# Attention on one Trainium2 core: the value products of a round in two PSUM banks instead of one, the first scores over all eight

## The chip, the cores and the metric

The kernel runs on one core of a Trainium2 chip. Its engines work side by side, each through its own list of instructions in order: TensorE (PE: matrix products and transposes, into PSUM), VectorE (DVE), ScalarE (ACT), GpSimd (POOL), and SyncE (SP), which here only issues DMAs. PSUM has eight banks of 2 KB in each of 128 partitions; the kernel names them h0 to h3 and y0 to y3. The metric is the device time of one execution in microseconds (us). The kernel before takes 863.77 us (median of three runs, 863.53 to 864.34).

## The reference

What is computed is an attention with a causal window of 128 positions, followed by two feed-forward layers:

```
scores = q k^T / 8 - slope_h * |i - j|   for 0 <= i - j < 128, else -1e9   (4 batches, 8 heads, 576 positions, 64 wide)
attn   = softmax(scores); x = attn v            -> x: 2304 tokens x 512
x      = (x w_in) * cos(x w_in) w_out           (512 -> 2048 -> 512)
out    = gate(x w_in') w_out'                   (the same sizes, a piecewise square)
```

All of it is in fp32. The change touches only how the attention is laid out in PSUM and in what order its steps are issued.

## The kernel before

**Pairs and rounds.** The 2304 tokens are 18 blocks of 128. A *pair* is two neighbouring blocks (j = 0, 1) with two heads (h = 0, 1); there are 36 pairs, and two of them (k = 0, 1) make a *round*: 18 rounds, r = 0 to 17. For a pair the kernel does the following.

1. `score`: four matmuls, q of block j against the 256 (at a sequence's start 128) keys before it. The scores of one head lie in one bank, those of block 0 in its columns 0 to 255, those of block 1 behind them. Then for each j and h a DVE operation (L493) adds the distance table, takes the row's extreme and writes the scores to SBUF (a tile `sc`), and ACT takes the exponential in place (L498).
2. `normal`: a sum gets 1e-9 added (L506), DVE takes the reciprocal (L507), and POOL multiplies the scores by it (L517), one instruction for each block.
3. `turn_round`: PE transposes each block's `sc` (L534) into a bank, and DVE or ACT copies that to SBUF (L541, a tile `pt`; of three copies two on DVE).
4. `output`: PE multiplies `pt` by v (L559). The result is x. For the first 768 tokens (pairs 0 to 11, so rounds 0 to 5) it stays in SBUF as a rounded high part (ACT, L577) and the remainder (DVE, `sub_lo` at L296), the second from the first; for later tokens one engine copies it (L587) and SP stores it.

**Order on PE.** It is the order of the program: in turn r come the scores of round r (banks y0 to y3), the products with v of round r-2 (both pairs in bank h3, pair 1 behind pair 0), and the transposes of round r-1 (h0, h1 for pair 0; h2, h3 for pair 1). Turn r is the stretch from one round's scores to the next round's. The scores of round 0 alone lie in h0 to h3.

**Order on the other engines.** A planner (`Plan.order`, with a cost and a latency for each operation in `COST`) runs the whole program through a model and fixes the order in which DVE, ACT, POOL and SP get their instructions. Operations depend on each other by resources: a bank, a buffer, and before the change also the two column ranges of a bank as resources of their own (`p["part"]`, `parts`). Semaphores are set by the layer below, by tiles of PSUM.

**After the attention** the feed-forward layers begin with `mm_a` (L754) into h0, h1 and h3, their activations (L763 to L778) and `mm_b` (L793); the last two products with v and the last transposes lie between these. From there on the kernel is a long row of 128x128x384 matmuls (L870, L942, L1031), with weights decoded on ACT and DVE, stored and loaded again (`wq`).

Of the kernel before, what the change touches and what calls it, by code (L numbers as in the profile page):

```python
# [9 lines left out]
F32 = mybir.dt.float32  # L10
# [247 lines left out]
def attention_moe_moe_kernel(  # L258
# [40 lines left out]
    def big(tag, bufs, name, dtype=F32R, shape=(128, 2, 512)):  # L299
        return two.tile(list(shape), dtype, tag=tag, name=nm(name), bufs=bufs)  # L300
# [129 lines left out]
    def attention(plan, bank, x_res, sin_ready, stat, dist_held):  # L430
# [3 lines left out]
        for name in ("straddle", "after"):  # L434
            for i in range(2):
# [17 lines left out]
        def stats(p, a, b):  # L453
            return stat.t.rearrange("p k n -> p (k n)")[:, 12 * p["n"] + a:12 * p["n"] + b]

        def used(o):
            if o not in stat.users:
                stat.users.append(o)
            return o
# [4 lines left out]
            p[name] = b = Buf("B", lambda: big("B", 14, name, F32, (128, 2 * HT)))  # L464
            op("S", name, lambda: SP.dma_start(b.t[:, 0:c.stop - c.start], qkv[p["b0"] // 2, p["hp"], :, c]), writes=[b], gate=gate)

        def score(p, j, tags, first):
            w = p["w"][j]
            kc = 256 + (j + 2) * 128 - w
            if j == 0:  # L470
                p["bank"] = [Cell(), Cell()]
                p["part"] = [[Res(), Res()] for _ in range(2)]
            cells, b = p["bank"], p["qk"]

            def go():
                for h in range(2):
                    if j == 0:
                        cells[h].t = ps.tile([128, 512], F32, tag=tags[h], name=nm("pa"))
                for h in range(2):
                    r = slice(64 * h, 64 * h + 64)  # L480
                    PE.matmul(cells[h].t[:, 256 * j:256 * j + w], lhsT=b.t[r, j * 128:j * 128 + 128],  # L481
                              rhs=b.t[r, kc:kc + w], start=True, stop=True)

            o = op("PE", "s+" if first else "s", go, reads=[b],
                   writes=[*p["part"][j], *([bank[t] for t in tags] if j == 0 else [])])
            sc = Buf("s", lambda: small("sc", shape=(128, 2, 256)))
            p["sc", j] = sc, [Half(sc), Half(sc)]
            for h in range(2):
                part = lambda: cells[h].t[:, 256 * j:256 * j + w]
                area = lambda h=h: cells[h].t[:, 256 * j:256 * j + w]  # L490
                res = p["part"][j][h]
                c = 2 * j + h
                o = op("D", f"max{w}", lambda a=area, h=h, c=c: DVE.tensor_tensor_reduce(  # L493
                    out=sc.t[:, h, 0:w], in0=a(), in1=dist8[p["kind"][j], 2 * p["hp"] + h][:, 256 - w:256], scale=-0.125,
                    scalar=3.0e38, op0=ALU.add, op1=ALU.min, accum_out=stats(p, c, c + 1)),
                    reads=[res, bank[tags[h]], *far.get((p["kind"][j], p["hp"] // 2), ())], writes=[p["sc", j][1][h]])
                maxes.append(used(o))
                exps.append(used(op("A", f"exp{w}", lambda h=h, c=c: ACT.activation(  # L498
                    sc.t[:, h, 0:w], sc.t[:, h, 0:w], AF.Exp, bias=stats(p, c, c + 1), scale=-1.0,
                    accum_out=stats(p, 4 + c, 5 + c)), writes=[p["sc", j][1][h]])))  # L500

        def normal(p, near):
            g = exps[-4:]
# [20 lines left out]
        def turn_round(p, j, tag, first, e=None):  # L524
            nb, n = p["w"][j] // 128, 2 * p["w"][j]
            sc, hs = p["sc", j]
            cell = Cell()

            def go():
                cell.t = ps.tile([128, 512], F32, tag=tag, name=nm("pa"))  # L530
                for h in range(2):
                    for i in range(nb):
                        c = (h * nb + i) * 128
                        PE.transpose(cell.t[:, c:c + 128], sc.t[:, h, i * 128:i * 128 + 128], ident)  # L534

# [5 lines left out]
            op(e, f"pt{n}", lambda: f(b.t[:, 0:n], cell.t[:, 0:n]), reads=[bank[tag]], writes=[b])  # L541

        moved = [0]

        def output(ps_, tag, e=None):
            cell, parts = Cell(), [Res(), Res()]
            for k, p in enumerate(ps_):

                def go(k=k, p=p):
                    if k == 0:  # L550
                        cell.t = ps.tile([128, 512], F32, tag=tag, name=nm("pa"))
                    for j in range(2):
                        nb = p["w"][j] // 128
                        for i in range(nb):
                            for h in range(2):
                                vc = (j + 2 - nb + i) * 128 + 64 * h
                                c = (h * nb + i) * 128
                                o = 256 * k + 128 * j
                                PE.matmul(cell.t[64 * h:64 * h + 64, o:o + 128],  # L559
                                          lhsT=p["v"].t[:, vc:vc + 64], rhs=p["pt", j].t[:, c:c + 128],  # L560
                                          start=(i == 0), stop=(i == nb - 1))

                op("PE", "v" if k else "v+", go, reads=[p["v"], p["pt", 0], p["pt", 1]],
                   writes=[parts[k], *([] if k else [bank[tag]])])
            for k, p in enumerate(ps_):
                src = lambda k=k: cell.t[:, 256 * k:256 * k + 256]
                t0, hp = p["b0"] * 128, p["hp"]
                if t0 < CH:
                    i = int(t0 >= FIRST[1][0])
                    c = t0 - FIRST[i][0]  # L570
                    hi, lo = Res(), Res()
                    x_res[i, hp] += [hi, lo]

                    def high(i=i, hp=hp, c=c, src=src):
                        if (i, hp) not in x0:
                            new_x0(i, hp)
                        ACT.copy(x0[i, hp][0][:, c:c + 256], src())  # L577

                    op("A", "x256", high, reads=[parts[k], bank[tag]], writes=[hi])
                    op("D", "x256", lambda i=i, hp=hp, c=c, src=src: sub_lo(  # L580
                        DVE, x0[i, hp][1][:, c:c + 256], src(), x0[i, hp][0][:, c:c + 256]),
                        reads=[parts[k], bank[tag], hi], writes=[lo])
# [4 lines left out]
                op(f, "x256", lambda x=x, f=f, src=src: (ACT.copy if f == "A" else DVE.tensor_copy)(x.t, src()),  # L587
                   reads=[parts[k], bank[tag]], writes=[x])
# [701 lines left out]
```

## Time and profile before

| what | value |
|---|---|
| median of three runs | 863.77 us (863.53 to 864.34) |
| the profiled execution | 864.19 us, span 862.1 us |
| PE / DVE / ACT / POOL busy over the span | 98% / 83% / 75% / 10% |
| attention, from round 0's scores to those of round 17 | 4.03 to 102.76 us |

The profile is of one execution. The span is what the profiler recorded, 2.1 us less than that execution's time. PE is busy for nearly all of the span; what is left to gain on waits is the rest, and where PE waits can be read from the idle time ahead of an instruction and what released it.

### The profile page before, as it was taken

What the parts mean: (1) busy time and instruction counts of PE and PEld (TensorE: products, weight loads), DVE (VectorE), ACT (ScalarE), POOL (GpSimd) and SP (SyncE); (2) the same over time, 40 slices, a digit from 0 to 9 for tenths busy, and PEclk for the clock granted to TensorE, in tenths of its full rate; (3) what the DMA queues carried; (4) which work ended last, traced back from release to release, by engine and by line L of the source; (5) the groups of instructions that cost most, each with busy time, mean ns of one, the idle gap of its engine ahead of it and who ended that gap; (6) DMA issues with size and microseconds to landing.
All of it is one profiled execution on the core that took longest, in us unless ns stands there. A gap on an engine that the chain in (4) does not pass through costs nothing.

```text
span 862.1 us, 16046 instructions
## 1 busy us (share of the span) xinstructions
PE 846.5 (98%) x5376; PEld 812.0 (94%) x5376; DVE 717.6 (83%) x1657; ACT 644.1 (75%) x1430; POOL 83.0 (10%) x118
## 2 busy tenths in 40 slices
PE   6999999999999999999999999999999999999998
PEld 5778878888889999999999999999999999999998
DVE  6889899899878998989888977877779999488954
ACT  6899878999857787677777767775488866488652
POOL 4877730000000000000000000000000000000000
PEclk9999999999999999999999999999999999999999
DMA  8678646785789998679889599999499898887861
GB/s 322 190 230 280 192 160 230 247 281 192 264 300 360 354 385 308 241 275 356 275 307 345 188 335 339 382 373 328 135 310 337 316 357 294 296 283 268 314 211 56
DMA packets 107730, 241.71 MB, mean 280 GB/s; under 512 B 10368, under 2 KB 57472, under 8 KB 107648
## 3 DMA queue, kind: packets, MB, share of 16 engines
q1 hardware_dynamic: 107648, 240.69, 79.7%
q8 instruction: 43, 0.70, 0.3%
q14 instruction: 39, 0.32, 0.1%
HBM read 174.59 MB, written 63.96 MB: 277 GB/s over the span
## 4 chain that ended last, share of the span: by engine, by line
PE 93%; DVE 3%; ACT 2%; POOL 1%; issue 1%; DMA 0%; POOLq 0%; ACTq 0%; DVEq 0%
PE h L870 34%; PE y L942 23%; PE y L1031 13%; PE y L793 8%; PE h L754 7%; PE pa L481 3%; PE pa L559 2%; PE pa L534 2%; DVE sc L493 1%; ACT sc L498 1%; POOL sc L517 1%; DVE pt L541 0%; DMA qk<-in_qkv 0%; ACT x L577 0%; DVE x L296 0%
## 5 line engine op out<-in xcount | busy, mean ns | idle before, releaser
L870 PE MATMUL h<-b,wq 128*128 128x384 f32 x1680 | 302.0, 334 | 0.6 <-ACT c L878 0.6
L870 PEld LDWEIGHTS h<-b,wq 128*128 128x128 f32 x1680 | 292.0, 188 | 1.0 <-ACT c L878 0.9
L942 PE MATMUL y<-gh,wo 128*128 128x384 f32 x768 | 203.4, 334 | 0.0
L942 PEld LDWEIGHTS y<-gh,wo 128*128 128x128 f32 x768 | 139.5, 188 | 0.0
L942 PE MATMUL y<-gl,wo 128*128 128x384 f32 x384 | 128.3, 334 | 0.0
L1031 PE MATMUL y<-gs,wq 128*128 128x384 f32 x672 | 118.1, 334 | 0.0
L1031 PEld LDWEIGHTS y<-gs,wq 128*128 128x128 f32 x672 | 116.6, 188 | 0.0
L883 DVE TENSOR_TENSOR c<-h,c 128x384 f32<-128x384 f32 x136 | 75.0, 555 | 39.6 <-ACT c L878 24.7
L878 ACT COPY c<-h 128x384 f32<-128x384 f32 x120 | 57.3, 478 | 51.2 <-PE h L870 49.9
L498 ACT ACTIVATE sc<-sc,up 128x256 f32<-128x256 f32 (+1 forms) x144 | 70.1, 488 | 13.9 <-DVE up L493 12.5
L1059 ACT CAST gs<-g 128x384 fp32r<-128x384 f32 x96 | 49.3, 513 | 33.9 <-PE y L1031 31.7
L517 POOL TENSOR_TENSOR sc<-sc,up 128x512 f32<-128x512 f32 (+1 forms) x71 | 70.8, 1019 | 26.1 <-DVE up L507 21.2
L754 PE MATMUL h<-x,wi 128*128 128x512 f32 (+1 forms) x384 | 72.2, 338 | 0.1
L942 PEld LDWEIGHTS y<-gl,wo 128*128 128x128 f32 x384 | 72.1, 188 | 0.0
L754 PEld LDWEIGHTS h<-x,wi 128*128 128x128 f32 x384 | 60.0, 190 | 8.3 <-ACT x L587 0.3
L296 DVE TENSOR_TENSOR gs<-g,gs 128x384 fp32r<-128x384 f32 x96 | 53.4, 557 | 16.6 <-ACT gs L1059 16.3
L493 DVE CUSTOM_DVE_ANT_0 sc<-pa,dist 128x256 f32<-128x256 f32 (+1 forms) x144 | 50.5, 402 | 8.1 <-PE pa L481 8.0
L903 ACT ACTIVATE t<-t,values 128x384 f32<-128x384 f32 x64 | 39.3, 615 | 11.5 <-DVE t L900 10.5
L296 DVE TENSOR_TENSOR so<-up,so 128x512 fp32r<-128x512 f32 x64 | 41.7, 655 | 3.7 <-ACT so L334 3.6
L534 PE MATMUL pa<-ident,sc 128*128 128x128 f32 x272 | 36.8, 281 | 6.8 <-POOL sc L517 2.8
L667 ACT ACTIVATE wst<-wst 128x512 int32<-128x512 uint16 x64 | 42.7, 670 | 0.0
L675 DVE TENSOR_SCALAR wst<-wst 128x512 uint16<-128x512 uint16 x55 | 42.3, 773 | 0.5
(96 smaller groups left out, 1345.1 us busy)
## 6 DMA issues: line engine op xcount, KB each, us to landing
wq<-fd SPq DMA_DIRECT2D x120, 512.0 KB, 5.8
wst<-in_w SPq DMA_DIRECT2D x64, 512.0 KB, 4.9
wq<-foM SPq DMA_DIRECT2D x56, 512.0 KB, 5.3
fd<-so SPq DMA_DIRECT2D x40, 512.0 KB, 5.4
qk<-in_qkv SPq DMA_DIRECT2D x36, 320.0 KB, 4.0
wq<-fd SPq DMA_DIRECT2D x40, 256.0 KB, 5.4
foM<-so SPq DMA_DIRECT2D x32, 256.0 KB, 6.0
xs<-xd SPq DMA_DIRECT2D x40, 192.0 KB, 5.4
```

The source lines that it names most:

```text
L296: eng.tensor_tensor(out=out, in0=full, in1=f32(hi), op=ALU.subtract)
L493: o = op("D", f"max{w}", lambda a=area, h=h, c=c: DVE.tensor_tensor_reduce(out=sc.t[:, h, 0:w], in0=a(), in1=dist8[p["kind"][j], 2 * p["hp ...
L498: exps.append(used(op("A", f"exp{w}", lambda h=h, c=c: ACT.activation(sc.t[:, h, 0:w], sc.t[:, h, 0:w], AF.Exp, bias=stats(p, c, c + 1), s ...
L517: used(op("P", f"norm{2 * w}", lambda sc=sc, j=j, w=w: POOL.tensor_tensor(out=sc.t[:, :, 0:w], in0=sc.t[:, :, 0:w], in1=stats(p, 8 + 2 * j ...
L534: PE.transpose(cell.t[:, c:c + 128], sc.t[:, h, i * 128:i * 128 + 128], ident)
L754: PE.matmul(h, lhsT=wi[f].t[:, k, s], rhs=x, start=(n == 0), stop=(n == 11))
L793: PE.matmul(y_of[i][d], lhsT=wo[0][f].t[:, a, s], rhs=part(x), start=(f == 0 and k == 0 and not (i and d % 2)), stop=(f == NF - 1 and k == ...
L870: PE.matmul(cell.t, lhsT=unit.t[:, a, s], rhs=bs[kt].t[:, x, :], start=(start and i == 0), stop=(stop and i == 5), skip_group_check=True)
L878: op("A", "copy384", lambda: ACT.copy(s.t, cell.t), reads=[bank[tag]], writes=[s])
L883: op("D", "tt384", lambda: DVE.tensor_tensor(out=to.t, in0=cell.t, in1=s.t, op=ALU.add), reads=[bank[tag], s] if new else [bank[tag]], wri ...
L942: PE.matmul(cell.t, lhsT=w[:, a, s], rhs=x.t, start=(first and i == 0 and k == 0), stop=(last and i == 1 and k == 2), skip_group_check=True)
L1031: PE.matmul(cells[i].t, lhsT=w.t[:, k, a, i * 128:i * 128 + 128], rhs=g.t[x], start=(start and n == 0), stop=(stop and n == 2), skip_group ...
```

## The change

`score` now makes both blocks of a pair at once. In every round but the first the banks are used as before, but the two column ranges are no resources of their own: each reader depends on the whole bank. In round 0 each block has two banks of its own, pair 0 in y0 to y3, pair 1 in h0 to h3. `output` puts the two pairs' products in two banks, h2 and h3 (in the last round h2 and h1). The two `pt` tiles of a pair become halves of one tile from the pool `Q`, which the weights of the first layer use too, and no longer take two of the 14 tiles of pool `B`. Costs and rules of the planner stay.

```diff
-        def score(p, j, tags, first):
-            w = p["w"][j]
...
-            o = op("PE", "s+" if first else "s", go, reads=[b],
-                   writes=[*p["part"][j], *([bank[t] for t in tags] if j == 0 else [])])
...
-                    reads=[res, bank[tags[h]], *far.get((p["kind"][j], p["hp"] // 2), ())], writes=[p["sc", j][1][h]])
+        def score(p, tags, first):
+            b, cells, parts = p["qk"], {}, {}
+            whole = len(tags) == 2
+            for j in range(2):
...
+                at = 256 * j * whole
...
+                mine = tags if whole else tags[2 * j:2 * j + 2]
...
+                op("PE", "s+" if first and j == 0 else "s", go, reads=[b], writes=[bank[t] for t in mine])
+            for j in range(2):
...
+                        reads=[bank[mine[h]], *edge], writes=[p["sc", j][1][h]])))
...
-            p["pt", j] = b = Buf("B", lambda: big("B", 14, "pt", F32, (128, 2 * HT)))
+            if j == 0:
+                p["pt"] = b = Buf("Q", lambda: big("Q", Q_BUFS, "pt", F32))
+                p["pt", 0], p["pt", 1] = Half(b), Half(b)
...
-        def output(ps_, tag, e=None):
-            cell, parts = Cell(), [Res(), Res()]
+        def output(ps_, tags):
+            cells = [Cell() for _ in ps_]
...
-                op("PE", "v" if k else "v+", go, reads=[p["v"], p["pt", 0], p["pt", 1]],
-                   writes=[parts[k], *([] if k else [bank[tag]])])
+                op("PE", "v" if k else "v+", go, reads=[p["v"], p["pt", 0], p["pt", 1]], writes=[bank[tags[k]]])
...
-                    op("A", "x256", high, reads=[parts[k], bank[tag]], writes=[hi])
+                    op("A", "x256", high, reads=[bank[tags[k]]], writes=[hi])
...
         def scores(r):
-            tags = YT if r else H_T
             for k, p in enumerate(rounds[r]):
-                for j in range(2):
-                    score(p, j, tags[2 * k:2 * k + 2], j == 0 and k == 0)
+                score(p, YT[2 * k:2 * k + 2] if r else (YT, H_T)[k], k == 0)
...
-                output(rounds[r - 2], "h3")
+                output(rounds[r - 2], ("h2", "h3"))
...
-        output(rounds[nr - 2], "h3")
+        output(rounds[nr - 2], ("h2", "h3"))
...
-        output(rounds[nr - 1], "h2")
+        output(rounds[nr - 1], ("h2", "h1"))
```

Three places show what moves. On PE, in turn 4, the products of round 2 and the transposes of round 3; a `pa` with one number is one bank. Before:

```order
L559 MATMUL pa_573<-pt_532,v_277 64x128 x4
L559 MATMUL pa_573<-pt_534,v_277 64x128 x4
L559 MATMUL pa_573<-pt_544,v_284 64x128 x4
L559 MATMUL pa_573<-pt_550,v_284 64x128 x4
L534 MATMUL pa_610<-ident,sc_456 128x128 x4
L534 MATMUL pa_616<-ident,sc_468 128x128 x4
L534 MATMUL pa_624<-ident,sc_485 128x128 x4
L534 MATMUL pa_632<-ident,sc_488 128x128 x4
```

And now:

```order
L567 MATMUL pa_574<-pt_530,v_281 64x128 x8
L567 MATMUL pa_592<-pt_534,v_288 64x128 x8
L541 MATMUL pa_607<-ident,sc_468 128x128 x4
L541 MATMUL pa_617<-ident,sc_473 128x128 x4
L541 MATMUL pa_623<-ident,sc_487 128x128 x4
L541 MATMUL pa_634<-ident,sc_499 128x128 x4
```

The order of the work is the same; the products lie in two banks (574 in h2, 592 in h3), and the third transposes (623) use the bank of the first product, the fourth (634) that of the second. On DVE, in the same turn, from the last operations on the scores of round 4 on (`x` the remainders of round 2, `pt` the copies of round 3's transposes, `up` the sums and reciprocals). Before:

```order
L493 ISA sc_589,up_218<-pa_559,dist_294 128x256
L493 ISA up_218 128x1
L296 TENSOR_TENSOR x_408<-pa_573,x_407 128x256
L296 TENSOR_TENSOR x_418<-pa_573,x_417 128x256
L541 COPY pt_629<-pa_610 128x512
L541 COPY pt_638<-pa_616 128x512
L541 COPY pt_647<-pa_632 128x512
L507 RECIPROCAL up_218<-up_218 128x4 x2
```

And now:

```order
L296 TENSOR_TENSOR x_409<-pa_574,x_408 128x256
L500 ISA sc_601,up_218<-pa_561,dist_301 128x256
L500 ISA up_218 128x1
L296 TENSOR_TENSOR x_419<-pa_592,x_418 128x256
L551 COPY pt_628<-pa_607 128x512
L551 COPY pt_628<-pa_617 128x512
L514 RECIPROCAL up_218<-up_218 128x4
L551 COPY pt_639<-pa_634 128x512
```

The first remainder stands ahead of the last score operation, and a reciprocal ahead of the third copy. On SP, far behind the attention, in the second layer (`wq` loads of weights, `foM` stores of sums of weights). Before:

```order
L303 DMA foM_179<-so_8563 128x2x256
L303 DMA wq_8607<-fd_6_3_131 128x2x256
L303 DMA wq_8621<-fd_7_0_132 128x1024
L303 DMA foM_163<-so_8582 128x2x256
L303 DMA foM_179<-so_8582 128x2x256
```

And now:

```order
L303 DMA foM_179<-so_8541 128x2x256
L303 DMA foM_163<-so_8554 128x2x256
L303 DMA foM_179<-so_8554 128x2x256
L303 DMA wq_8595<-fd_6_3_131 128x2x256
L303 DMA wq_8608<-fd_7_0_132 128x1024
```

Two stores now stand ahead of two loads.

## Rows read from the trace of the kernel before

**Rows 1.** The page: busy time of the engines over the span.

```profile
PE 846.5 (98%) x5376; PEld 812.0 (94%) x5376; DVE 717.6 (83%) x1657; ACT 644.1 (75%) x1430; POOL 83.0 (10%) x118
```

**Rows 2.** Waits of PE, 4 to 124 us: engine, line, releaser, total, times, longest.

```profile
PE pa L534 <- POOL sc L517: 2.8, 5, 0.8
PE pa L534 <- DVE x L296: 1.8, 4, 0.5
PE pa L534 <- DVE up L507: 1.5, 2, 0.9
PE pa L534 <- ACT x L587: 0.7, 2, 0.5
```

**Rows 3.** Waits of PE, 124 to 862 us.

```profile
PE h L870 <- ACT c L878: 0.6, 1, 0.6
```

**Rows 4.** PE in order of time: start, us, line, shapes [idle before, releaser].

```profile
13.96 2.95 PE L481 MATMUL pa<-qk 64*128 64x256 f32 x16
...
20.34 0.63 PE L534 MATMUL pa<-ident,sc 128*128 128x128 f32 x4 [0.94 <-DVE up L507]
...
28.82 1.97 PE L559 MATMUL pa<-pt,v 128*64 128x128 f32 x32
30.72 1.53 PE L534 MATMUL pa<-ident,sc 128*128 128x128 f32 x12
32.67 0.63 PE L534 MATMUL pa<-ident,sc 128*128 128x128 f32 x4 [0.43 <-DVE x L296]
...
109.34 0.66 PE L534 MATMUL pa<-ident,sc 128*128 128x128 f32 x4 [0.79 <-POOL sc L517]
...
121.76 1.97 PE L559 MATMUL pa<-pt,v 128*64 128x128 f32 x32 [0.59 <-ACT pt L541]
```

**Rows 5.** Stretches: length; busy of PE, PEld, DVE, ACT, POOL; granted clock; DMA.

```profile
18.05:31.85 13.80, 12.34 (x132) 10.15 (x129) 11.49 (x52) 12.39 (x46) 12.71 (x18) 1.00 0.67 215
26.89:33.23 6.34, 5.91 (x65) 4.90 (x65) 5.11 (x22) 5.76 (x22) 4.80 (x7) 1.00 0.61 170
33.23:39.63 6.40, 5.91 (x65) 4.90 (x64) 6.05 (x25) 4.83 (x18) 4.48 (x6) 1.00 0.76 266
39.63:45.97 6.34, 5.92 (x65) 4.90 (x64) 5.15 (x22) 6.17 (x22) 4.51 (x6) 1.00 0.52 164
45.97:52.38 6.41, 5.92 (x66) 4.90 (x65) 5.52 (x24) 5.83 (x22) 4.56 (x6) 1.00 0.56 167
85.59:91.32 5.73, 5.73 (x66) 4.93 (x65) 5.30 (x23) 5.60 (x20) 4.56 (x7) 1.00 0.80 239
13.00:14.00 1.00, 1.00 (x7) 0.67 (x5) 0.86 (x3) 0.79 (x4) 0.05 (x1) 0.50 1.07 402
```

**Rows 6.** ACT in order of time, turn 4.

```profile
30.83 0.37 ACT L577 CAST x<-pa 128x256 fp32r<-128x256 f32 x1 [0.17 <-PE pa L559]
...
31.70 0.37 ACT L577 CAST x<-pa 128x256 fp32r<-128x256 f32 x1
```

**Rows 7.** DVE in order of time, turn 4 and behind the attention.

```profile
31.24 0.42 DVE L296 TENSOR_TENSOR x<-pa,x 128x256 fp32r<-128x256 f32 x1 [0.16 <-ACT x L577]
32.10 0.42 DVE L296 TENSOR_TENSOR x<-pa,x 128x256 fp32r<-128x256 f32 x1 [0.44 <-ACT x L577]
32.44 1.88 DVE L541 COPY pt<-pa 128x512 f32<-128x512 f32 x3
...
123.01 0.42 DVE L769 TENSOR_TENSOR t<-h,t 128x256 f32<-128x256 f32 x1
```

**Rows 8.** POOL in order of time, from turn 2 to turn 5.

```profile
18.05 1.61 POOL L517 TENSOR_TENSOR sc<-sc,up 128x256 f32<-128x256 f32 x2 [2.19 <-DVE up L507]
...
29.81 2.04 POOL L517 TENSOR_TENSOR sc<-sc,up 128x512 f32<-128x512 f32 x2 [0.30 <-DVE up L507]
...
34.55 4.03 POOL L517 TENSOR_TENSOR sc<-sc,up 128x512 f32<-128x512 f32 x4 [0.70 <-DVE up L507]
```

**Rows 9.** The page: DMA issues, KB each, us from issue to landing.

```profile
wq<-fd SPq DMA_DIRECT2D x120, 512.0 KB, 5.8
```

More of the change, by code (lines that the diff above doesn't have):

```diff
@@ L465, in fetch @@
             op("S", name, lambda: SP.dma_start(b.t[:, 0:c.stop - c.start], qkv[p["b0"] // 2, p["hp"], :, c]), writes=[b], gate=gate)
-        def score(p, j, tags, first):
-            w = p["w"][j]
[L469 to L475, printed above, removed]
-                for h in range(2):
-                    if j == 0:
-                        cells[h].t = ps.tile([128, 512], F32, tag=tags[h], name=nm("pa"))
-                for h in range(2):
-                    r = slice(64 * h, 64 * h + 64)
-                    PE.matmul(cells[h].t[:, 256 * j:256 * j + w], lhsT=b.t[r, j * 128:j * 128 + 128],
-                              rhs=b.t[r, kc:kc + w], start=True, stop=True)
-            o = op("PE", "s+" if first else "s", go, reads=[b],
-                   writes=[*p["part"][j], *([bank[t] for t in tags] if j == 0 else [])])
[L486 to L495, printed above, removed]
-                    reads=[res, bank[tags[h]], *far.get((p["kind"][j], p["hp"] // 2), ())], writes=[p["sc", j][1][h]])
[L497 to L500, printed above, removed]
@@ new lines, in score, with go @@
+        def score(p, tags, first):
+            b, cells, parts = p["qk"], {}, {}
+            whole = len(tags) == 2
+            for j in range(2):
+                w = p["w"][j]
+                kc = 256 + (j + 2) * 128 - w
+                at = 256 * j * whole
+                for h in range(2):
+                    if j == 0 or not whole:
+                        cells[j, h] = Cell()
+                    else:
+                        cells[j, h] = cells[0, h]
+                mine = tags if whole else tags[2 * j:2 * j + 2]
+                def go(j=j, w=w, kc=kc, at=at, mine=mine):
+                    for h in range(2):
+                        if j == 0 or not whole:
+                            cells[j, h].t = ps.tile([128, 512], F32, tag=mine[h], name=nm("pa"))
+                    for h in range(2):
+                        r = slice(64 * h, 64 * h + 64)
+                        PE.matmul(cells[j, h].t[:, at:at + w], lhsT=b.t[r, j * 128:j * 128 + 128],
+                                  rhs=b.t[r, kc:kc + w], start=True, stop=True)
+                op("PE", "s+" if first and j == 0 else "s", go, reads=[b], writes=[bank[t] for t in mine])
+            for j in range(2):
+                w = p["w"][j]
+                at = 256 * j * whole
+                mine = tags if whole else tags[2 * j:2 * j + 2]
+                sc = Buf("s", lambda: small("sc", shape=(128, 2, 256)))
+                p["sc", j] = sc, [Half(sc), Half(sc)]
+                edge = far.get((p["kind"][j], p["hp"] // 2), ())
+                for h in range(2):
+                    c = 2 * j + h
+                    maxes.append(used(op("D", f"max{w}", lambda j=j, h=h, c=c, w=w, at=at, sc=sc: DVE.tensor_tensor_reduce(
+                        out=sc.t[:, h, 0:w], in0=cells[j, h].t[:, at:at + w],
+                        in1=dist8[p["kind"][j], 2 * p["hp"] + h][:, 256 - w:256], scale=-0.125,
+                        scalar=3.0e38, op0=ALU.add, op1=ALU.min, accum_out=stats(p, c, c + 1)),
+                        reads=[bank[mine[h]], *edge], writes=[p["sc", j][1][h]])))
+                    exps.append(used(op("A", f"exp{w}", lambda h=h, c=c, w=w, sc=sc: ACT.activation(
+                        sc.t[:, h, 0:w], sc.t[:, h, 0:w], AF.Exp, bias=stats(p, c, c + 1), scale=-1.0,
+                        accum_out=stats(p, 4 + c, 5 + c)), writes=[p["sc", j][1][h]])))
@@ L577, in high @@
                         ACT.copy(x0[i, hp][0][:, c:c + 256], src())
-                    op("A", "x256", high, reads=[parts[k], bank[tag]], writes=[hi])
+                    op("A", "x256", high, reads=[bank[tags[k]]], writes=[hi])
                     op("D", "x256", lambda i=i, hp=hp, c=c, src=src: sub_lo(
                         DVE, x0[i, hp][1][:, c:c + 256], src(), x0[i, hp][0][:, c:c + 256]),
-                        reads=[parts[k], bank[tag], hi], writes=[lo])
+                        reads=[bank[tags[k]], hi], writes=[lo])
                     continue
@@ L587, in output @@
                 op(f, "x256", lambda x=x, f=f, src=src: (ACT.copy if f == "A" else DVE.tensor_copy)(x.t, src()),
-                   reads=[parts[k], bank[tag]], writes=[x])
+                   reads=[bank[tags[k]]], writes=[x])
                 o = t0 % CH
```

13 lines of the change are left out of this document (6 added, 7 removed).

## The prediction, as it was put on record before the changed kernel ran

> **What bounds the kernel now.** I read the busy times first: PE is busy for 98% of the span [rows 1], so the time is PE's work plus the few places where PE waits. The waits of PE by releaser come next, in two stretches. From 124 us to the end there is one of 0.6 us [rows 3]; what comes behind the attention waits for nothing that a bank could free, so whatever the attention saves should reach the end whole. Up to 124 us PE waits for POOL's normalised scores (2.8 us in 5 waits), and ahead of transposes for the eviction of x: for DVE's remainders (1.8 in 4), for ACT's copies of x (0.7 in 2), and twice for a DVE reciprocal (1.5), which in both places is only what DVE did right behind a remainder [rows 2]. PE in order of time shows the place: in turns 2 to 7 the stall sits ahead of the fourth transposes of the turn, those of pair 1, block 1 [rows 4], and these write bank h3, where both products with v lie until they are evicted.
>
> The bank is held for long because its four readers go one after another. In turn 4 the products start at 28.82 and the transposes behind them at 30.72 [rows 4]. ACT's first cast comes at 30.83, released by PE, which is after both products, though the first needs only half of the 1.90 us. DVE's first remainder follows at 31.24 with 0.16 us of idle time ahead of it, ACT's second cast at 31.70, DVE's second remainder at 32.10 with 0.44 us idle ahead, each time for ACT [rows 6, 7]. PE's fourth transposes begin at 32.67 after 0.43 us [rows 4]. So DVE isn't late: it waits for ACT, and ACT for the bank.
>
> A turn without the stall takes 5.73 us with PE busy for all of it; turns 4 to 7 take 6.34, 6.40, 6.34 and 6.41 [rows 5].
>
> **The change part by part.**
>
> *Products in two banks.* PE runs the same instructions. The first product is complete 0.95 us earlier than the pair (half of 30.72 - 28.82), so its cast and remainder can run while PE makes the second product and the first two transposes. New waits come with it. The third transposes (h2) wait for the first pair's remainder; behind them on PE stand the fourth transposes and the next scores, for which DVE and POOL wait. If the remainders came as late as now, the first would be done at 31.24 + 0.42 = 31.66, when the third transposes are due (30.72 plus half of 1.90): such a wait is at most some 0.1 us, and I take 0, because the new order has that remainder ahead of DVE's last score operation. The fourth would be due at 32.15 (30.72 plus three quarters of 1.90). With a cast at 30.83, now for pair 1, its remainder is through by 31.24 + 0.42, so the bank is no longer last.
>
> The gain if nothing else is late: turns 4 to 7, (6.34 + 6.40 + 6.34 + 6.41) - 4 x 5.73 = 2.57 us [rows 5]. In these turns PE counts as busy for 5.91, 0.18 more than 5.73, so a stall costs its idle time and 0.18 more. For turns 2 and 3: 1.5 idle, the two waits put down to a reciprocal [rows 2], + 0.36 = 1.86. For the two stalls on ACT's x, in turns 9 and 11: 0.7 + 0.36 = 1.06. Together 5.5 us, the upper end for this part; the lower end is 0, if another wait stands right behind each.
>
> *What is late next.* In turns 2 to 4 that is POOL. From 18.05 to 31.85 it is busy for 12.71 of 13.80 us [rows 5], and its last normalisation of round 3 runs from 29.81 to 31.85 [rows 8], 0.3 us before the fourth transposes are due even without the gains of turns 2 and 3. It can only move with its start, 18.05, which a DVE reciprocal releases [rows 8]; the new order issues that reciprocal one score operation earlier, some 0.35 us. With 0.2 from the start (below) POOL ends at 31.3, and the transposes begin at about 31.4 in place of 32.67: 1.27 us for turns 2 to 4 and the start together, in place of 1.86 + 0.61 + 0.2.
>
> In turns 5 to 7 POOL has idle time (0.70 us ahead of 34.55 [rows 8]). But round 4's normalisation ends at 34.55 + 4.03 = 38.58, and in turn 5 the fourth transposes are due without a stall at 33.23 + (32.15 - 26.89) = 38.49. It starts late because its reciprocal stands behind three copies of 1.88 us together on DVE [rows 7]; the new order puts it behind two, 0.6 us earlier. I count three quarters of the 1.96 us of turns 5 to 7, 1.5, and the same share of turns 9 and 11, 0.8.
>
> *Round 0 in eight banks.* DVE's first operation waits for two matmuls in place of four, and round 1's scores now wait for round 0's readers, in banks that these leave early. No row has this alone. It is bounded by 0 and by the POOL waits of the first transposes, part of the 2.8 us [rows 2]; a small loss is possible too, if round 1's scores come late. POOL is what releases those transposes, and its reciprocals stand behind operations on round 1's scores that keep their places, so I take 0.2.
>
> *Whole-bank dependencies.* Of what is issued nothing changes; the planner counts on scores of both blocks together. I give it 0 apart from the moved reciprocals. They also bear on the end of the attention, where PE waits 0.79 us for POOL ahead of 109.34 [rows 4] with a reciprocal behind a row of copies: 0.4, between 0 and 0.79.
>
> *The last product in h1.* It must wait until the first layer's activation has read h1. In the trace that reading ends at 123.01 + 0.42 [rows 7], and the second half of the products begins at 121.76 + 0.98 [rows 4]: a wait of 0.7 us if the order stayed. The new order has it ahead of the two copies of transposes that the products themselves wait for, so I take 0; behind it on PE stand the first `mm_b`.
>
> *`pt` in pool Q, and loads.* The copies are the same instructions. Loads of q, k and v wait less, since `pt` leaves their pool; the first layer's weights share Q with `pt` and are decoded later, still ahead of their use. 0, bounded by 0.6 either way, the only wait behind 124 us [rows 3].
>
> Sum: 1.27 + 1.5 + 0.8 + 0.4 = 4.0 us. The profiled execution took 864.19 us, 2.1 of them outside the span, which nothing here touches; that gives 860.2. It lies 0.42 above the median of the runs, so the forecast for the median is 863.77 - 4.0 = 859.8.
>
> **The rivals.**
>
> *POOL's chain takes the bank's place throughout.* From round 4's scores (26.89) to the end of its normalisation (38.58) pass 11.69 us. A turn of 5.73 has the transposes due 5.73 + 5.26 = 10.99 after the scores, so the 0.7 us by which the chain is longer are the stall itself. For it: ACT and DVE, which feed POOL, are busy for 5.76 and 5.11 us of turn 4 [rows 5]. Against it: the turn from 85.59 runs in 5.73 with ACT at 5.60 and DVE at 5.30, so the engines can. Then turns 5 to 11 give some 0.6 us in place of 2.3: 863.77 - 2.3 = 861.5. Chance 0.25.
>
> *The clock at the start stays high.* Between 13 and 14 us the granted clock is 0.50, the lower level of 1.2 GHz, after PE had stood idle in pieces ahead of the first transposes; round 2's scores then take 2.95 us [rows 4, 5] in place of the 1.93 of turn 4's (26.89 to 28.82). Less idle time there could keep the clock at 2.4 GHz and save about 1.3 us more: 858.5. POOL still sets those pieces, so 0.08. The Trainium skill ("TensorE: Matmul & The Clock Gate", What's actually happening) says that the low clock is the default and that activity releases it; by that rule the gaps need only shrink enough, and the trace agrees so far that the clock fell behind gaps.
>
> *The bank was not what held PE.* If the semaphores let the second product be read no earlier than now, or DVE reaches the remainders late anyhow, the stalls stay, and the rest gives 0.5: 863.3. Against it stand DVE's idle 0.16 and 0.44 us ahead of the remainders [rows 7], which together are the 0.61 of a stall. 0.08.
>
> *Slower: a load of weights too late.* The planner's order moves to the end of the program. In the second layer SP now has two stores of sums ahead of two `wq` loads; a store waits until ACT and DVE have written its source, and all loads queue behind it. A load lands 5.8 us after its issue [rows 9]. If PE reaches weights whose load was just issued, it waits up to 5.8 us, more than the whole gain: 859.8 + 5.8 = 865.6. It decides once the store holds SP for longer than the load has in hand; that PE waits for no DMA behind 124 us [rows 3] speaks for a lot in hand. 0.06.
>
> **How the numbers follow.** The forecast, 859.8, has the remaining 0.53; its own bounds are 5.5 + 0.2 + 0.8 with all of the terms (857.3) and 2.3 (861.5). The range for 8 in 10 runs from 857.6, short of all terms, to 863.0, near the case in which only the start gains. What this measurement can tell from no change is about 0.2%, 1.7 us. Faster by more: 0.53 + 0.08 + 0.17 of the POOL case = 0.78. Within it: the rest of the POOL case and most of the third rival, 0.15. Slower: the last rival and a rest, 0.07.
>
> **What would show it.** In the profile after, the fourth transposes of turns 4 to 7 should follow the third with no wait for a DVE remainder, and turns of 6.34 to 6.41 us should be 5.7 to 5.9; the second cast on ACT should no longer wait for DVE. If POOL took over, PE's waits for L517 in the attention grow from 2.8 us to 4 or more. PE's waits behind 124 us should stay at about 0.6; a DMA among them would show the slower case. I am wrong in the main step if the turns keep 6.3 us, and wrong in the cover if they shorten and the end does not come earlier by as much.

## The result and the profile after

The changed kernel took 856.89 us (median of 4 runs, 856.33 to 857.54) beside 863.73 us for the kernel before (863.53 to 864.34) on the same chip: 0.992 of the time, interval 0.9903 to 0.9937. It is faster, as forecast, but by 6.8 us where 4.0 were forecast, and lies 0.7 us below the range.

In some runs of either kernel the granted clock of PE is 0.50 for about 3.4 us between 11 and 17 us and the run is mostly 1.3 to 1.8 us longer, so I also give the median of the runs with a mean clock of 0.999 or more, "at full clock". For the kernel before that is 862.1 us (56 of the 92 runs that it made beside the experiments; the other 36 have a median of 863.7), for the changed one 856.3 (f1 below). Like to like the change is worth 5.8 us.

PE's busy time on the page of the changed kernel (answers to [rows 1]):

```profile
PE 843.3 (99%) x5376; PEld 810.6 (95%) x5376; DVE 716.3 (84%) x1657; ACT 643.1 (75%) x1430; POOL 83.4 (10%) x118
```

PE's waits of the changed kernel from 4 to 120 us (line, releaser: total, times, longest), to be held against [rows 2]; the first row is the wait for the first load:

```profile
PE pa L487 <- DMA qk<-in_qkv: 4.1, 1, 4.1
PE pa L541 <- POOL sc L524: 2.8, 6, 0.7
PE pa L541 <- DVE x L296: 0.3, 1, 0.3
```

The waits for ACT's copies of x and for reciprocals are gone. So are the four for DVE's remainders in turns 4 to 7; the one that is left lies in turn 2, where the wait before was put down to a reciprocal. Those for POOL are 2.8 us as before. From 118 us to the end PE waits as in [rows 3]:

```profile
PE h L875 <- ACT c L883: 0.6, 1, 0.6
```

The last products with v begin at 114.20 in place of 121.76, and from there to the end of the span it is 740.3 us in both (862.1 - 121.76, 854.5 - 114.20). So the 7.56 us between the two profiled executions arise ahead of the last products and nothing is given back.

PE of the changed kernel in order of time (start, us, idle before and releaser), against [rows 4]:

```profile
12.71 2.00 PE L487 MATMUL pa<-qk 64*128 64x256 f32 x16
...
23.47 0.66 PE L541 MATMUL pa<-ident,sc 128*128 128x128 f32 x4 [0.33 <-POOL sc L524]
...
25.98 1.97 PE L567 MATMUL pa<-pt,v 128*64 128x128 f32 x32
27.88 2.14 PE L541 MATMUL pa<-ident,sc 128*128 128x128 f32 x16
...
52.39 0.66 PE L541 MATMUL pa<-ident,sc 128*128 128x128 f32 x4 [0.34 <-POOL sc L524]
...
102.84 0.66 PE L541 MATMUL pa<-ident,sc 128*128 128x128 f32 x4 [0.35 <-POOL sc L524]
...
114.20 1.97 PE L567 MATMUL pa<-pt,v 128*64 128x128 f32 x32
```

All 16 transposes of turn 4 now stand in one row without a wait. The same stretches as in [rows 5], turns 4 to 8 and the microsecond at 13 (length; busy PE, PEld, DVE, ACT, POOL; granted clock; DMA):

```profile
24.05:29.95 5.90, 5.90 (x65) 4.90 (x65) 5.23 (x24) 5.54 (x22) 5.26 (x8) 1.00 1.04 392
29.95:35.67 5.72, 5.72 (x65) 4.92 (x64) 5.36 (x25) 4.90 (x20) 4.63 (x7) 1.00 0.68 212
35.67:41.40 5.73, 5.73 (x66) 4.93 (x65) 5.05 (x23) 5.65 (x21) 4.55 (x7) 1.00 0.58 181
41.40:47.12 5.72, 5.72 (x65) 4.92 (x65) 5.52 (x23) 5.72 (x22) 4.37 (x6) 1.00 0.84 263
47.12:52.98 5.86, 5.52 (x66) 4.72 (x65) 5.17 (x24) 5.86 (x25) 4.52 (x6) 1.00 0.27 87
13.00:14.00 1.00, 1.00 (x12) 0.89 (x12) 0.98 (x4) 0.53 (x4) 0.63 (x2) 1.00 1.08 402
```

Turns 5 to 7 took 19.15 us before and take 17.17 now; turn 8 grew from 5.30 to 5.86. In turn 4, ACT's casts of x against [rows 6]:

```profile
27.25 0.35 ACT L584 CAST x<-pa 128x256 fp32r<-128x256 f32 x1
...
28.00 0.36 ACT L584 CAST x<-pa 128x256 fp32r<-128x256 f32 x1
```

and DVE's remainders against [rows 7]:

```profile
27.70 0.42 DVE L296 TENSOR_TENSOR x<-pa,x 128x256 fp32r<-128x256 f32 x1
...
28.40 0.42 DVE L296 TENSOR_TENSOR x<-pa,x 128x256 fp32r<-128x256 f32 x1
```

The first cast starts 1.27 us behind the start of the products (25.98), before 2.01, and none of the four shows a wait. POOL in turns 4 and 5, against [rows 8]:

```profile
26.27 3.04 POOL L524 TENSOR_TENSOR sc<-sc,up 128x512 f32<-128x512 f32 x3
...
30.25 1.04 POOL L524 TENSOR_TENSOR sc<-sc,up 128x512 f32<-128x512 f32 x1 [0.64 <-DVE up L514]
31.38 0.22 POOL L513 TENSOR_SCALAR up<-up 128x4 f32<-128x4 f32 x1
31.68 3.04 POOL L524 TENSOR_TENSOR sc<-sc,up 128x512 f32<-128x512 f32 x3
```

Round 4's normalisation ends at 34.72, that is 10.67 us behind its scores (24.05); before it was 11.69, and 10.99 is what a turn without a stall allows. DVE's second remainder, the other thing that the fourth transposes wait for, came earlier too, and by more: in turn 5 it ended 5.71 us behind the turn's start (38.52 + 0.42 - 33.23) and now ends 4.77 behind it (34.30 + 0.42 - 29.95). Nothing that the fourth transposes of turns 5 to 7 wait for is late any more.

### The profile page after: what moved, and what is told of

The parts are those of the page before. It is cut to its first block, busy times and chain, and to the rows that moved or that the text cites. A ratio compares the mean times of both kernels' runs of the same rounds, so it can differ in the third digit from the quotient of the medians.

```text
span 854.5 us, 16042 instructions
## 1 busy us (share of the span) xinstructions
PE 843.3 (99%) x5376; PEld 810.6 (95%) x5376; DVE 716.3 (84%) x1657; ACT 643.1 (75%) x1430; POOL 83.4 (10%) x118
## 4 chain that ended last, share of the span: by engine, by line
PE 94%; DVE 2%; POOL 2%; issue 1%; ACT 0%; DMA 0%; POOLq 0%
PE h L875 34%; PE y L947 23%; PE y L1036 14%; PE h L759 8%; PE y L798 8%; PE pa L487 3%; PE pa L541 2%; PE pa L567 2%; POOL sc L524 2%; DVE sc L500 1%; ACT sc L505 0%; DMA qk<-in_qkv 0%; DVE pt L551 0%; DVE c L888 0%; DVE x L296 0%
## 5 line engine op out<-in xcount | busy, mean ns | idle before, releaser
L296 DVE TENSOR_TENSOR gl<-t,gh 128x384 fp32r<-128x384 f32 (+1 forms) x64 | 37.6, 587 | 6.4 <-ACT gh L894 4.3
```

Source lines behind the costliest of these rows:

```text
L296: eng.tensor_tensor(out=out, in0=full, in1=f32(hi), op=ALU.subtract)
```

## The experiments

All ran beside the kernel before, whose median at full clock was within 0.2 us on each of the chips used, so the column "at full clock" can be compared across rows. Three theories: the bank held PE; the planner's other order did it (above all the place of the reciprocals, through POOL); the eight banks of round 0 did it through the start and the clock. "Turn" is from one round's scores to the next one's on PE.

| run | median us | ratio (95%) | at full clock | turns 4 to 7, us | turn 17, us |
|---|---|---|---|---|---|
| before | 862.1 to 862.7 | | 862.1 | 6.34 6.40 6.34 6.41 | 6.99 |
| f1 changed, again | 856.27 | 0.9924 (0.9912-0.9937) | 856.3 | 5.90 5.73 5.72 5.72 | 6.11 |
| e1 two banks alone | 860.70 | 0.998 (0.997-0.999) | 860.5 | 5.95 6.24 5.95 6.24 | 7.26 |
| e2 eight banks alone | 863.47 | 1.0013 (1.0002-1.0024) | 862.9 | 6.33 6.42 6.34 6.36 | 8.23 |
| e3 two banks, old order | 861.69 | 0.9983 (0.9974-0.9991) | 860.6 | 5.95 6.24 5.94 6.25 | 7.27 |
| e4 one bank, new order | 862.56 | 0.9993 (0.9984-1.0001) | 861.7 | 6.34 6.34 6.33 6.34 | 6.74 |
| f2 without eight banks | 856.82 | 0.9935 (0.9922-0.9949) | 856.8 | 5.72 5.72 5.72 5.73 | 6.11 |
| f3 pt in the old pool | 858.99 | 0.9958 (0.9945-0.9970) | 859.0 | 5.90 6.13 5.72 6.25 | 6.97 |
| f4 e1, reciprocals due earlier | 860.12 | 0.9975 (0.9964-0.9985) | 859.7 | 5.95 6.24 5.95 7.22 | 5.80 |
| g1 e3, reciprocals up | 859.59 | 0.9971 (0.9960-0.9982) | 859.4 | 5.94 6.25 5.95 6.24 | 6.13 |
| g2 g1, remainders up | 861.09 | 0.9978 (0.9968-0.9987) | 859.7 | 5.95 6.25 5.95 6.46 | 6.11 |
| g3 changed, reciprocals down | 861.39 | 0.9987 (0.9978-0.9996) | 861.4 | 5.90 6.13 5.97 5.97 | 6.82 |
| g4 changed, remainders down | 856.34 | 0.9931 (0.9918-0.9943) | 856.3 | 5.96 5.72 5.72 5.73 | 6.11 |
| h1 before, reciprocals up | 861.43 | 0.9990 (0.9981-1.0000) | 861.3 | 6.34 6.40 6.34 6.41 | 6.38 |
| h2 g1, POOL's order too | 861.05 | 0.9984 (0.9973-0.9996) | 861.0 | 5.96 7.03 5.95 6.25 | 6.54 |
| h3 changed, reciprocals up | 855.55 | 0.9928 (0.9914-0.9942) | 855.5 | 5.91 5.72 5.73 5.72 | 5.67 |

**One part alone (e1, e2).** e1 adds only this to the kernel before, e2 only the new `score` with round 0's eight banks:

```
-            cell, parts = Cell(), [Res(), Res()]
+            cells = [Cell() for _ in ps_]
...
-                output(rounds[r - 2], "h3")
+                output(rounds[r - 2], ("h2", "h3"))
```

> The kernel before with one part of the change: the two products with v of a round lie in banks h2 and h3 (those of the last round in h2 and h1), planned anew. Theory (the bank is what held PE): turns 2 to 4 give 1.1 us, turns 5 to 7 1.4, turns 9 and 11 0.9, and some of the 1.9 us of the end of the attention, so 859 to 860.5 against 863.7 for the kernel before; PE's waits for DVE's remainders and ACT's casts ahead of transposes are gone. Rival (the other order, which whole-bank waits and eight banks give, does it): 863 or more, with the waits still there.

> The kernel before with the other part: the scores of round 0 lie over all eight banks, and scores are planned with whole-bank waits; the two products stay in one bank. Theory (the start and the clock are a matter of the eight banks): the first transposes come about 0.6 us earlier, the granted clock stays at 1.0 between 12 and 16 us, and the time is 861.5 to 862.3; the waits of turns 4 to 7 for x stay. Rival (only a little of the start goes, the clock falls as before): 863.3 to 863.8. Second rival (the order does all of it): 857 to 859.

e1 came out at 860.5 at full clock, as the bank theory has it, but turns 5 and 7 stay at 6.24 us. The profile puts their waits down to POOL's addition (0.33 us each), which the transposes do not read; what they wait for is shown under g1. e2 is no faster, and 0.8 us slower at full clock: the stalls of turns 4 to 7 remain, its turn 17 takes 8.23. Its clock fell in 3 of 11 runs, so the eight banks do not keep the clock up. The parts give -1.6 and +0.8, the change -5.8: they don't add up. The third part, `pt` in pool Q, is in neither of them (f3 below is without it). Of the 4.1 us by which the profiled execution of e1 is behind the changed kernel's at the last products (118.26, 114.20), 1.3 lie in turns 4 to 7 and 1.7 in turn 17 and behind it.

**Bank against order (e3, e4).** The planner is told of one layout, the tiles are allocated in the other, so every instruction keeps its place:

```
-                    cells[k].t = ps.tile([128, 512], F32, tag=tags[k], name=nm("pa"))
+                    if k == 0:
+                        one_cell.t = ps.tile([128, 512], F32, tag=tag, name=nm("pa"))
```

> The order of the kernel before, instruction by instruction, but the two products lie in banks h2 and h3 (the last round's stay in one). If the bank by itself held PE: PE stops waiting ahead of the fourth transposes, turns 4 to 7 go from 6.35 to 5.8 to 6.1 us, and the time is 860.5 to 862. If the order is what counts: the fourth transposes wait for something else or the third ones for the first remainder, and the time is 863.5 or above.

> The order of the changed kernel, instruction by instruction, but both products lie in one bank again (h3, the last round's in h2). If the bank by itself held PE: the waits for x ahead of the fourth transposes come back, and the time is 859.5 to 861.5. If the order counts: 857 to 858.

Old order with two banks: 860.6. New order with one bank: 861.7, PE in turns 4 and 5 (start, us, idle before and releaser):

```profile
30.07 0.63 PE L541 MATMUL pa<-ident,sc 128*128 128x128 f32 x4 [0.43 <-DVE x L296]
...
36.41 0.63 PE L541 MATMUL pa<-ident,sc 128*128 128x128 f32 x4 [0.42 <-DVE x L296]
```

This is the stall of turn 4 in [rows 4], 0.43 us, in the new order. So one bank holds PE, whatever the order; but in the old order two banks bring back only a part. Two banks give 1.5 us in the old order and 5.4 in the new one; the order gives 0.4 in one bank and 4.3 in two. "New order" here is the changed kernel's with all of its parts, the eight banks of round 0 too.

**The changed kernel less one part (f1 to f3).** f2 puts round 0 back into four banks, f3 puts `pt` back into the pool of q, k and v:

```
-                score(p, YT[2 * k:2 * k + 2] if r else (YT, H_T)[k], k == 0)
+                score(p, (YT if r else H_T)[2 * k:2 * k + 2], k == 0)
...
-                p["pt"] = b = Buf("Q", lambda: big("Q", Q_BUFS, "pt", F32))
+            p["pt", j] = b = Buf("B", lambda: big("B", 14, "pt", F32, (128, 2 * HT)))
```

> The changed kernel itself, again, beside the kernel before on the same chip, for the groups of times. The kernel before fell into two groups, some 862.1 us with a granted clock of 1.000 and some 863.7 with 0.998. If the clock at the start belongs to the run and not to the kernel, the changed kernel has both groups too, about 1.3 us apart (856.4 and 857.6 or so), and like to like the change is 5.7 to 6.1 us. If the eight banks keep the clock up, all of its runs lie at 856.4.

> The changed kernel with one part undone: round 0's scores lie in four banks, two for a pair, as before. Theory (the eight banks give only some tenths at the start): the first 8.61 us up to round 2's scores become about 8.95, all later turns stay, 856.8 at the clock of 1.0. Rival (the eight banks set the order of the first rounds, and POOL's chain in turns 2 to 8 starts later): 858 or more, with turns 4 to 8 of 5.9 or more.

> The changed kernel with one part undone: pt in a tile for each block in the pool of q, k and v, as before, not halves of one tile of Q. In the order planned for it the reciprocal of turn 5 stands behind three copies of transposes again, as in the kernel before, and not behind two. Theory (POOL's chain, set by the place of the reciprocal, is what is late once the bank is free): turns 5 and 7 take about 6.2 us in place of 5.72, so 857.3 to 858.5. Rival (the place of the reciprocal does not count, nor the pool): 856.4, turns of 5.72.

f1's five runs all have the full clock, which alone would speak for eight banks that keep it up. But one of the first four runs of the same kernel took 857.5 us at a mean clock of 0.998, and e2, e4, g3, g4 and h3, with eight banks too, have such runs: 12 of 58 runs of kernels with eight banks, 69 of 167 with four. So the eight banks do not keep the clock up; whether they make its fall rarer is not shown. f2: by the medians of four and five runs the eight banks are worth 0.5 us. The traces don't show where: up to round 2's scores f2 took 8.79 us and f1 8.89, and turns 3 and 4 together take 11.75 in f2 and 11.73 in f1. f3 came out above its bounds, for a reason that I had only half: turns 5 and 7 take 6.13 and 6.25, as expected of the reciprocal behind three copies (in turn 7 the second remainder was as late as POOL), and turn 17 takes 6.97, but turns 8 to 11 are shorter by 0.7. Another wait makes up the rest, PE's waits of f3 from 118 us:

```profile
PE h L872 <- DMA wq<-fd: 1.9, 1, 1.9
```

This is the mechanism of my slower rival, a weight load issued too late after a new plan, in a sibling of the changed kernel.

**Moving single instructions (f4, g1 to g4, h1 to h3).** f4 plans e1 anew with `o.late -= 1.0` for each reciprocal. The others take the finished order and move only single instructions on DVE (h2 one on POOL as well), all else in place. The move up of g1 and the move on POOL of h2; "down" is the reverse, h1 to h3 move only the first of two reciprocals in a row, and g2 and g4 move remainders past a score operation in the same way:

```
+        if RECIP and d[i].cost == "recip" and d[i - 1].cost == "pt512" and d[i].start > 17:
+            d[i - 1], d[i] = d[i], d[i - 1]
...
+        if p[i].cost == "add" and p[i + 1].cost == "norm512" and p[i - 1].cost == "add" and p[i].start > 17:
+            p[i], p[i + 1] = p[i + 1], p[i]
```

> The kernel with two banks for the products alone (860.5 at the clock of 1.0), and the planner's due time of each reciprocal 1.0 us earlier: in turns 5 and 7 it then stands on DVE behind two copies of transposes in place of three. Theory (after the bank it is the reciprocal's place, through POOL): turns 5 and 7 go from 6.24 to 5.75 to 5.95, so 859.5 to 860. Rival (the remaining stall of these turns is ACT's or the scores' order): 860.5, turns of 6.24.

f4 settled nothing: the new plan moved more than the reciprocals, and turn 7 got a wait of 1.3 us for a copy of transposes.

> The order of the kernel before and two banks for the products (860.6 at the clock of 1.0), and on DVE alone one more move: each reciprocal that stands right behind a copy of transposes goes ahead of that copy (from turn 2 on; turns 5 and 7 among them). Every other instruction keeps its place. Theory (POOL's chain is the next limit and the reciprocal sets it): turns 5 and 7 go from 6.24 us to 5.7 to 5.95, the time to 859.6 to 860.1. Rival (the remainder of the first pair, which still stands behind all maxima, holds the bank as long): 860.4 to 860.7, and PE waits for DVE's x in these turns in place of POOL.

> The same, and the first pair's remainder goes ahead of the last maximum of its turn as well (turns 3 to 8), as in the changed kernel. Theory (bank, reciprocal and remainder together are the mechanism): turns 4 to 7 of 5.72 to 5.9 us, the time 859.0 to 859.6; what is then left to the changed kernel (856.3) is the start, turns 2 and 3, and the end of the attention. Rival (remainders do not count): the time of the run with the reciprocals alone.

g1's time is about what was expected, for another reason than expected: turns 5 and 7 keep 6.25 and 6.24, and turn 17 goes from 7.27 to 6.13. POOL of g1 at the start of turn 5, then DVE and PE at its end:

```profile
32.53 0.22 POOL L541 TENSOR_SCALAR up<-up 128x4 f32<-128x4 f32 x1 [0.97 <-ACT sc L533]
32.85 4.04 POOL L552 TENSOR_TENSOR sc<-sc,up 128x512 f32<-128x512 f32 x4
...
36.64 0.69 DVE L576 COPY pt<-pa 128x512 f32<-128x512 f32 x1
37.25 0.41 DVE L331 TENSOR_TENSOR x<-pa,x 128x256 fp32r<-128x256 f32 x1
...
37.81 0.63 PE L569 MATMUL pa<-ident,sc 128*128 128x128 f32 x4 [0.33 <-DVE up L542]
```

In the old order POOL's addition for the second pair stands ahead of the first pair's normalisation and waits for ACT's last exponential. I took that for the reason (h2 tests it), but it is not: the normalisation ends at 36.89, 0.92 us before the fourth transposes begin. DVE's second remainder ends at 37.66, 0.15 before them, as in turn 4 of the kernel before (32.10 + 0.42 and 32.67 [rows 4, 7]), while transposes that wait for POOL begin 0.05 or 0.06 us after its end (23.42 and 23.47 in turn 3 of the changed kernel). The same gap of 0.14 or 0.15 us stands behind the second remainder in each of turns 4 to 7 of e1, e3, g1, g2 and h2. So with two banks in the old order it is still the second product's bank that PE waits for. In turns 5 and 7 its remainder stands on DVE behind a copy of transposes of 0.69 us; in the changed kernel it stands ahead of the copies. g2 moves the first pair's remainders, not these, and brings nothing more.

> The changed kernel, and on DVE alone each reciprocal that stands right ahead of a copy of transposes goes behind that copy, 0.6 us later (from turn 3 on). Theory (POOL's chain is what is late next and the reciprocal sets it): turns 3, 5, 8 and others that had no time in hand grow by 0.2 to 0.5 us, the time is 857.3 to 858.8, and PE's waits for POOL grow by as much. Rival (the bank alone was the change): 856.3.

> The changed kernel, and on DVE alone the first pair's remainder goes behind the last maximum of its turn, 0.35 us later (turns 3 to 8), as it stood before. Theory (the remainder's place is a part of the gain, since the third transposes of the turn wait for the first bank): PE waits 0.2 to 0.35 us for DVE's x ahead of the third transposes in 4 to 6 turns, each 0.2 to 0.5 us longer, 857.3 to 858.5. Rival (the two transposes ahead hide it): 856.3 to 856.6.

g3 is the clearest run: moves of 0.6 us on DVE alone cost 5.1 of the 5.8 us, far more than I expected. PE's waits of g3 from 4 to 120 us:

```profile
PE pa L576 <- POOL sc L559: 4.8, 11, 0.8
```

Six waits for POOL become eleven. g4: the remainder's place counts for nothing, against my expectation.

> The kernel before, both products in one bank, and on DVE alone the first reciprocal that stands right behind a row of copies of transposes goes ahead of the last of them (turns 2, 5, 7, 17 among them). Theory (the end of the attention gained by the reciprocal, not by the banks): turn 17 goes from 6.99 to 6.1 to 6.3 us and turns 4 to 7 keep 6.34 to 6.41, since their bank is held; 861.2 to 861.6 in place of 862.1. Rival (the end needs the banks): 862.1 and turn 17 of 6.99.

> The old order with two banks, the reciprocal ahead of one copy as in the run before with two banks (859.5 at the clock of 1.0, turns 5 and 7 of 6.24), and one more move, on POOL alone: where its addition for the second pair stands ahead of the first pair's first normalisation, it goes behind it, as in the changed kernel. Theory (in turns 5 and 7 POOL's queue made the reciprocal's move worth nothing, since the normalisation stood behind an addition that waits for ACT's last exponential): turns 5 and 7 go to 5.72 to 5.95, 858.6 to 859.2. Rival (something else holds these turns): 6.24, 859.5.

> The changed kernel, and on DVE alone each reciprocal that stands right behind a copy of transposes goes ahead of it (turns 3, 4, 8 and 17 among them, where PE waits 0.33 to 0.35 us for POOL). Theory (the same chain still sets these stalls): turn 8 goes from 5.86 towards 5.3 and turn 17 from 6.12 to 5.8, 855.3 to 855.9 in place of 856.3. Rival (DVE then waits for POOL's addition, and what is behind the reciprocal on DVE is late): 856.3 to 857.5.

The run h1 has turns 4 to 7 as before, to the hundredth, and turn 17 at 6.38 in place of 6.99: at the end of the attention the reciprocal gains alone, in one bank. h2 refutes its theory: with the addition behind the normalisation, DVE's second reciprocal waited 0.95 us for it with the next maxima queued behind, both remainders came later still, and turn 5 took 7.03. No run moves the second remainder ahead of the copy in the old order, so that this would give turns of 5.73 is likely by the traces, but not shown. h3 beats both kernels, by 0.8 us at full clock against the changed one (the intervals of their ratios overlap): turn 8 5.63, turn 17 5.67. PE's waits of h3 from 4 to 120 us:

```profile
PE pa L571 <- POOL sc L554: 1.2, 3, 0.5
```

## Why the prediction was right or wrong

**The bottleneck and the main step were right.** The bank held PE (e3, e4), the stall is gone from turns 4 to 7, and all of the gain reached the end. "The bank is no longer last" holds with the changed kernel's order alone: there the second remainder of turn 5 ends 0.42 us before the fourth transposes begin (34.72, 35.14), while in the old order it still ends last (g1). The step on what is late next, the place of the reciprocals through POOL, holds for the changed kernel; g3 and h3 show it from both sides. In turns 5 and 7 of the old order it was not POOL that ended PE's wait.

**The terms.** Measured from the two profiled executions, less 1.6 us of clock (863.7 - 862.1):

| term | forecast | measured |
|---|---|---|
| start and turns 2 to 4 | 1.27 | 1.75 |
| turns 5 to 7 | 1.5 | 1.98 |
| turn 8 | 0 | -0.56 |
| turns 9 to 16 | 0.8, in turns 9 and 11 | 0.93 |
| end of the attention | 0.4 | 1.93 |
| sum | 4.0 | 6.0 |

The first row is the start of turn 5's scores: 33.23 before, 29.95 after, 0.07 later start included, is 3.35, less 1.6. The start itself differs by some 0.3 us between runs. That the middle rows come to 2.35 us where 2.3 were forecast is in part luck: turns 5 to 7 gave all that I had as their most, turn 8 lost 0.56 that I had not looked for, and of the last 0.93 turn 9 gave 0.88 and turn 11 only 0.07.

**The step that failed is the end of the attention**, "0.4, between 0 and 0.79". It gave 1.93, beyond its upper bound: 0.87 in turn 17 and 1.06 from there to the last products (12.01 before, 10.95 after). I saw only the wait for POOL ahead of 109.34. The run h1 shows that the reciprocal alone takes 0.61 off turn 17 in one bank, g1 1.14 in two. The 1.06 is ACT's queue, which I had not read there. ACT in order of time, the kernel before:

```profile
114.57 1.28 ACT L626 ACT_TABLE_LOAD   x1
...
115.97 0.36 ACT L587 COPY x<-pa 128x256 f32<-128x256 f32 x1
...
121.13 1.06 ACT L541 COPY pt<-pa 128x512 f32<-128x512 f32 x2
```

and the changed kernel:

```profile
108.25 0.37 ACT L594 COPY x<-pa 128x256 f32<-128x256 f32 x1 [0.20 <-PE pa L567]
108.64 1.28 ACT L631 ACT_TABLE_LOAD   x1
...
113.00 0.59 ACT L551 COPY pt<-pa 128x512 f32<-128x512 f32 x1
```

Before, the copy of x that frees a bank for the first layer stood behind a table load of 1.28 us and the last copies of transposes stood at the end of the queue. Now the copy stands ahead of the load and a copy of transposes comes earlier: PE reaches the last transposes 0.40 us sooner, and the products behind them another 0.66. The 0.59 us that PE waited for that copy is in [rows 4]; I read it for the bank h1 and did not ask whether the wait itself would go. e4, with one bank, has the short end too (10.96), so the order alone gives it; two banks in the old order give 0.42 of it (e3, 11.59).

**The clock.** The rival "the clock stays high" was priced about right (1.3 us; 1.6 by the medians of the two groups), and is the other part of the miss, some 0.8 us (6.84 - 6.0): the four runs of the kernel before in the first comparison lie at the times of its lower clock, 863.5 and above, and two of the four of the changed kernel at those of its full clock. But the rival's cause is not borne out. I took the clock for a property of the kernel's start; the same kernel shows both, and the idle pieces ahead of the first transposes did not shrink: 0.71, 0.56 and 0.55 us in the trace before, whose clock fell, 0.70, 0.56 and 0.55 in the one after, whose clock did not. That kernels with eight banks show the fall less often (f1 above) leaves open that the start has a part in it. The rule that I cited for it, that activity releases the low clock's throttle (the Trainium skill, "TensorE: Matmul & The Clock Gate", What's actually happening), is not refuted, but no row here shows what differed between two runs of one kernel.

**The other rivals.** POOL did take the bank's place, but in single turns (3, 8, 17: 0.33 to 0.35 us), not throughout. "The bank was not what held PE" is refuted by e4. The late weight load did not come in the changed kernel, but did in f3. "Round 0 in eight banks", for which I took 0.2, was 0.5 by the medians (f2), within its bounds. That the remainder's place ahead of the last maximum keeps the third transposes from waiting, for which I took 0, was not needed (g4).

## What to carry to other kernels

Where a stall has a cause in one resource, ask which queue comes next and price the change with that queue's order: here a second bank was worth 1.5 us or 5.4, depending on the order of the other engines' queues, and in the better order moving reciprocals of 0.17 us behind one copy cost 5.1. A releaser that the profile names can be the wrong one: look what the waiting instruction reads and writes, and which of these ended just before it. When a planner makes the order anew, read the end of the stage on every engine's queue, not only the wait that PE shows; small gains and losses sit there, and a sibling of the same change got a 1.9 us wait for weights. Before two runs are subtracted, see whether both had the same granted clock.

## What the runs showed of the hardware that was not expected

- The granted clock of PE fell to 0.50 (1.2 GHz of 2.4) between 11 and 17 us in 36 of 92 runs of the kernel before, by their mean clock, and by their times in two of nine of the changed one. In the eight traces that have it (before, e3, f4, g1, g2, g3, h1, h2) the stretch differs in its start but not in its length. Of e3, a microsecond at a time (granted clock third from the end):

```profile
11.00:12.00 1.00, 0.78 (x4) 0.38 (x3) 1.00 (x6) 1.00 (x7) 0.61 (x1) 0.54 1.04 397
12.00:13.00 1.00, 0.95 (x5) 0.95 (x6) 1.00 (x4) 0.74 (x4) 0.37 (x1) 0.50 1.05 377
13.00:14.00 1.00, 1.00 (x5) 0.67 (x5) 0.80 (x3) 0.93 (x5) 0.49 (x1) 0.50 1.11 416
14.00:15.00 1.00, 1.00 (x10) 0.79 (x10) 0.32 (x1) 0.00 (x0) 1.00 (x2) 0.75 1.04 414
15.00:16.00 1.00, 1.00 (x12) 0.62 (x10) 0.84 (x5) 0.38 (x1) 0.34 (x2) 1.00 1.01 401
```

What is missing to 1.00 is 1.71 us here, and 1.70 or 1.71 in the other seven: so the stretch is 3.4 us long each time, and 1.6 us is what the medians show of it.
- A 128x4 addition on POOL takes 0.22 us and a 128x4 reciprocal on DVE 0.17, yet their places can lengthen turns of 5.7 us (g3): both stand in queues in order, and a wait in one holds what is queued behind it in the other (h2: 0.95 us on DVE became 0.8 us of a turn).
- PE's transposes begin 0.14 or 0.15 us after the end of the DVE operation that they wait for (all 20 in turns 4 to 7 of e1, e3, g1, g2 and h2), but 0.05 or 0.06 after the end of a normalisation on POOL (turns 3, 4, 8 and 17 of the changed kernel). That tells the two apart where the releaser's name does not.
